# A linear-attention kernel with a gated feed-forward: order and places from tables, narrower carried products, one-pass decay test

## The chip, the cores and the metric

The kernel runs on one core of a Trainium2 chip. A core has a matrix engine (TensorE, called PE in the profile, with its weight loads as PEld), a vector engine (VectorE, DVE), a scalar engine (ScalarE, ACT), GpSimd (POOL) and SyncE (SP), which here issues the transfers. Products are written to PSUM, eight banks of 128 x 512 floats, and read from there by VectorE and ScalarE. Each engine works through its own list of instructions in a fixed order and waits at semaphores. The metric is the time of one execution in microseconds.

## What is computed

```python
def _attn_ref(r, k, v, w, u):                 # 4 x 8 heads x 768 steps x 48
    state = np.zeros((B, H, D, D)); y = np.zeros_like(r)
    for t in range(S):
        kt, vt, rt, wt = (k[:, :, t], v[:, :, t], r[:, :, t], w[:, :, t])
        cur = np.einsum('bhd,bhe->bhde', u[None] * kt, vt)
        y[:, :, t] = np.einsum('bhd,bhde->bhe', rt, state + cur)
        state = wt[:, :, :, None] * state + np.einsum('bhd,bhe->bhde', kt, vt)
    return y

def _moe_ref(x, w_in, conv_w, w_out):         # 4 x 768 x 384, d_ff 1024
    h = np.maximum(x @ w_in, 0.0)
    conv_out = ...                            # along the steps, kernel 3, per channel
    gate = 1.0 / (1.0 + np.exp(-conv_out))
    return (h * gate @ w_out)
```

The result y, with the heads side by side, is the x of the second function. The decays w lie between 0.8 and 0.95. The three weight arrays arrive in double precision; the others are float.

## The kernel before

The 768 steps of each of the four batches are cut into six chunks of 128 steps, 24 chunks n in all. A chunk goes through stage_a and stage_b; a block of 384 steps (two a batch, eight in all) goes through block, once its chunks are there.

stage_a loads w, k, r and v of a chunk and turns w, k and r with PE (`tr`, line 700). VectorE forms running products of the decays (scans, lines 708 and 719) and scales k and r with them, into the tile kr (lines 716, 723). The last 16 of the 48 dimensions of each head sit apart; they are collected into the tile last, by products on line 733 in the first four chunks and by transfers (line 741) later. GpSimd forms r*k*u (z, lines 749, 751) and spreads its sums on the diagonal of the score tile pm (line 755). Line 765 turns the scaled keys back (kh). Two passes of ScalarE test that all decays lie in a safe range (line 774).

stage_b decays the old state s into sd (lines 801 and 804, VectorE) and copies it to sbd (line 809, ScalarE), forms the scores (line 817), copies their upper triangle into pm (line 822), forms the new state (lines 836, 840), and adds up the result in one bank: first the carried part, state times r (`carried`, line 856, in all chunks but the first of a batch), then the part within the chunk (`within`, line 872). The result goes to xT as a float part and a correction (lines 877, 878).

block multiplies by the weights: 64 hidden tiles (line 887: nine products each, three each of three parts), their gating by relu, convolution, sigmoid and product (lines 899 to 909), and 24 output tiles (line 916). Both weights are first converted from double precision, in 17 pieces, each of three operations of ScalarE, two of VectorE (lines 600, 603) and two of GpSimd (lines 605, 585), and are loaded a second time for a range test (lines 620, 623).

Every operation is only recorded (`op`) with the tiles that it reads and writes. Plan.run then lays all of them out with estimated lengths (LEN), ranks (RANKS), costs for a change of shape on PE (SWITCH) and limits on places (CAPS), engine by engine, and Plan.issue writes them out in the order found. Where PE would have nothing to do in the first 120 us of that estimate, it records a filler product (`warm`, line 552: 256 columns of the identity).

## Time and profile before

| | before |
|---|---|
| median of three runs | 382.7 us (381.83 to 382.95) |
| profiled execution | 381.93 us |
| its span, first to last instruction | 380.2 us |
| PE busy, instructions | 97%, 3431 |
| VectorE, ScalarE, GpSimd busy | 72%, 65%, 47% |
| read from and written to memory | 31.88 MB, 4.72 MB |

The profile is one execution. A busy share is the time in which an engine has at least one instruction under way, so side-by-side instructions count once; the mean of one instruction can therefore be longer than the distance between two. The time of a run is somewhat longer than the span.

### The profile page before, as it was taken

How to read it: one execution, taken by the hardware profiler on the slowest of the kernel's cores; microseconds unless marked ns; L12 is line 12 of the kernel's file. 1: busy time of each engine (PE TensorE's matmuls, PEld its weight loads, DVE VectorE, ACT ScalarE, POOL GpSimd, SP SyncE). 2: the span in 40 equal slices, each digit the busy share in tenths (PEclk: the TensorE clock that was granted, in tenths of full speed). 3: DMA queues.
4: the chain of work that ended last, by engine and by line, in shares of the span. 5: the costliest groups of instructions: out<-in, count | busy, mean ns of one | idle time of the engine just before them, and what ended most of it. 6: DMA issues, size and time to landing. Idle time of an engine off the chain costs nothing.

```text
span 380.2 us, 9086 instructions
## 1 busy us (share of the span) xinstructions
PE 368.9 (97%) x3431; PEld 320.4 (84%) x3431; DVE 272.8 (72%) x547; ACT 247.7 (65%) x656; POOL 177.0 (47%) x199
## 2 busy tenths in 40 slices
PE   8999999989999999999999999999999999999993
PEld 5878796878998778789977979898977997999993
DVE  1998699994999588896297576698858487276700
ACT  6464888996798536887377456785654565487821
POOL 6387388998456403464235425355243231234310
PEclk9999999999999999999999999999999999999999
DMA  8999945226553758574235222334512000100011
GB/s 169 256 279 245 229 101 146 86 44 185 123 116 66 178 103 219 114 229 129 56 91 117 44 48 46 71 92 93 114 52 67 0 20 4 41 22 21 22 43 47
DMA packets 113815, 39.24 MB, mean 103 GB/s; under 512 B 102349, under 2 KB 109286, under 8 KB 113766
## 3 DMA queue, kind: packets, MB, share of 16 engines
q1 hardware_dynamic: 113764, 38.61, 41.8%
q8 instruction: 28, 0.46, 0.5%
q14 instruction: 21, 0.17, 0.2%
q10 hardware_dynamic: 2, 0.00, 0.0%
HBM read 31.88 MB, written 4.72 MB: 96 GB/s over the span
## 4 chain that ended last, share of the span: by engine, by line
PE 79%; ACT 7%; DVE 5%; DMA 3%; POOL 3%; issue 2%; SPq 0%; DVEq 0%; POOLq 0%; ACTq 0%
PE bank L887 23%; PE bank L916 23%; PE bank L856 9%; PE bank L817 5%; PE bank L700 5%; PE bank L872 5%; PE bank L836 3%; DMA r<-in_r_dram 2%; PE bank L552 2%; PE bank L765 2%; POOL val L605 1%; PE bank L733 1%; ACT val L596 1%; ACT junk L774 1%; DVE a L901 1%
## 5 line engine op out<-in xcount | busy, mean ns | idle before, releaser
L916 PE MATMUL bank<-wo,gh 128*128 128x384 f32 x576 | 122.1, 345 | 0.3 <-POOL wo L585 0.3
L887 PE MATMUL bank<-xT,wi 128*128 128x386 f32 x576 | 122.0, 346 | 0.3 <-DVE xT L878 0.2
L909 POOL TENSOR_TENSOR gh<-g,gh 128x384 fp32r<-128x384 f32 x64 | 65.5, 1031 | 99.6 <-ACT gh L908 97.4
L887 PEld LDWEIGHTS bank<-xT,wi 128*128 128x128 f32 x576 | 100.1, 189 | 3.8 <-issue 1.5
L916 PEld LDWEIGHTS bank<-wo,gh 128*128 128x128 f32 x576 | 98.8, 188 | 3.1 <-issue 1.7
L901 DVE SCALAR_TENSOR_TENSOR a<-bank,cw,a 128x384 f32<-128x384 f32 x64 | 38.4, 610 | 24.7 <-ACT a L900 24.1
L755 POOL TENSOR_SCALAR_AFFINE_SELECT pm<-dg 128x1024 f32<-128x1024 f32 x24 | 26.7, 1114 | 48.7 <-PE bank L872 38.9
L899 ACT ACTIVATE bank<-bank 128x386 f32<-128x386 f32 x64 | 30.4, 478 | 24.8 <-PE bank L887 24.3
L905 ACT ACTIVATE a<-a 128x384 f32<-128x384 f32 x64 | 33.3, 523 | 16.1 <-DVE a L903 15.9
L906 DVE TENSOR_TENSOR g<-bank,a 128x384 f32<-128x384 f32 x64 | 34.7, 550 | 12.6 <-ACT a L905 11.7
L822 DVE COPY_PREDICATED pm<-upper,bank 128x512 f32<-128x512 int32 x48 | 33.9, 735 | 7.2 <-PE bank L817 7.2
L903 DVE SCALAR_TENSOR_TENSOR a<-bank,cw,a 128x384 f32<-128x384 f32 x64 | 38.3, 610 | 0.7
L900 ACT ACTIVATE a<-bank,cw 128x384 f32<-128x384 f32 x64 | 36.5, 580 | 1.3 <-DVE g L906 0.6
L749 POOL TENSOR_TENSOR z<-r,k 128x384 f32<-128x384 f32 x24 | 24.9, 1037 | 25.9 <-DMA r<-in_r_dram 15.6
L908 ACT CAST gh<-g 128x384 fp32r<-128x384 f32 x64 | 32.0, 511 | 7.2 <-DVE g L906 6.4
L708 DVE TENSOR_TENSOR_SCAN kr<-bank,one_end 128x387 f32<-128x387 f32 x24 | 22.9, 955 | 11.3 <-POOL z L751 6.9
L856 PE MATMUL bank<-kr,sbd 112*64 112x128 f32 (+1 forms) x240 | 29.2, 290 | 0.4 <-DVE pm L822 0.4
L872 PE MATMUL bank<-pm,v 128*32 128x128 f32 x384 | 26.1, 277 | 0.0
L872 PE MATMUL bank<-pm,vz 128*32 128x128 f32 x384 | 25.8, 274 | 0.0
L751 POOL TENSOR_TENSOR z<-z,ubc 128x384 f32<-128x384 f32 x24 | 24.2, 1010 | 1.1
L856 PEld LDWEIGHTS bank<-kr,sbd 112*64 112x64 f32 (+1 forms) x240 | 13.5, 122 | 13.1 <-issue 11.8
L872 PEld LDWEIGHTS bank<-pm,v 128*32 128x32 f32 x384 | 19.6, 109 | 4.5 <-issue 3.8
(103 smaller groups left out, 587.6 us busy)
## 6 DMA issues: line engine op xcount, KB each, us to landing
gh<-in_moe_w_out_dram SPq DMA_DIRECT2D x5, 1152.0 KB, 7.0
w<-in_w_dram SPq DMA_DIRECT2D x24, 192.0 KB, 3.1
k<-in_k_dram SPq DMA_DIRECT2D x24, 192.0 KB, 3.3
r<-in_r_dram SPq DMA_DIRECT2D x24, 192.0 KB, 3.7
v<-in_v_dram SPq DMA_DIRECT2D x24, 192.0 KB, 3.1
gh<-in_moe_w_in_dram SPq DMA_DIRECT2D x4, 1152.0 KB, 7.0
out_dram<-val SPq DMA_DIRECT2D x24, 192.0 KB, 1.9
last<-kr SPq DMA_DIRECT2D x120, 16.2 KB, 1.9
```

The lines of the kernel that those rows point to most:

```text
L822: op("DVE", "cp", lambda g=g: nc.vector.copy_predicated(out=pm.t[:, g], mask=upper.unsqueeze(1).to_broadcast([P, NP, L]), data=sc[g].t.rea ...
L856: nc.tensor.matmul(rows(a, w), lhsT=sbd.t[:, m, e:e + w], rhs=rt(m), start=(j == 0), stop=False, skip_group_check=True)
L872: nc.tensor.matmul(rows(a, 32), lhsT=lhs, rhs=pm.t[:, g, j, :], start=(c == 0 and i == 0), stop=(i == 3), skip_group_check=True)
L887: nc.tensor.matmul(t.t[:, 0:xs.stop - xs.start], lhsT=wi[:, m, a, f * P:(f + 1) * P], rhs=xT[:, x0 + m, c, xs], start=(m == 0 and j == 0), ...
L900: ("ACT", "mul", lambda: nc.scalar.mul(out=a(), in_=h(1), mul=cw[:, 1, fs]), [t, "cw"], [a1]),
L901: ("DVE", "stt", lambda: nc.vector.scalar_tensor_tensor(out=a(), in0=h(0), scalar=cw[:, 0, fs], in1=a(), op0=ALU.mult, op1=ALU.add), [t], ...
L903: ("DVE", "stt", lambda: nc.vector.scalar_tensor_tensor(out=a(), in0=h(2), scalar=cw[:, 2, fs], in1=a(), op0=ALU.mult, op1=ALU.add), [t], ...
L905: ("ACT", "sig", lambda: nc.scalar.activation(out=a(), in_=a(), func=AF.Sigmoid), [], [a1]),
L906: ("DVE", "gate", lambda: nc.vector.tensor_tensor(out=g.t[:, 0:width], in0=h(1), in1=a(), op=ALU.mult), [t, a1], [g]),
L908: ("ACT", "cast", lambda: nc.scalar.copy(out=part(0)[:, 0:width], in_=g.t[:, 0:width]), [g], [key]),
L909: ("POOL", "lo", lambda: nc.gpsimd.tensor_tensor(out=part(1)[:, 0:width], in0=g.t[:, 0:width], in1=part(0)[:, 0:width].bitcast(F32), op=AL ...
L916: nc.tensor.matmul(acc.t[:, 0:DM], lhsT=part(a)[:, tt * P:(tt + 1) * P], rhs=wo[:, f, c, :], start=(f == 0 and a + c == 0), stop=(f == FT ...
```

## The change

It replaces the planner by two tables: ORDER, the numbers of all 2134 operations and of six fillers in the order in which they are issued, and PLACES, which buffer each takes when it is first used. With it:

- the carried products are all of 32 columns, 12 a chunk instead of 8 of 64 or 32;
- one pass of ScalarE per chunk, the square of w - 0.875 from the turned decays in PSUM with its sum, tests the decays, with a copy of three columns per chunk for a test of the chunk's product of decays; four small operations compare both at the end;
- the first part of the decay of the state goes from VectorE to GpSimd (new line 675), the second from VectorE to ScalarE;
- twelve row-sized buffers (strips) serve what had its own: a, g, val, e, z and v; w, k and r share six, s and sd four; the ring of large buffers has six places instead of five; dA has one buffer instead of two; all eight banks serve every use;
- u is spread by a product in the table's order (new line 629).

The core of the diff:

```diff
-        for _, i in order:
-            if not isinstance(i, int):
-                self.warm(i)
-                continue
-            for b in ops[i][4]:
-                if b.kind.make and not b.made:
-                    b.t, b.made = b.kind.make(), True
-            ops[i][2]()
+        done, places = set(), iter(PLACES)
+        for i in ORDER:
+            if i < 0:
+                self.warm(self.spare[-1 - i])
+                continue
+            _, _, f, deps, bufs = self.ops[i]
+            assert deps <= done
             for b in bufs:
                 if b.t is None:
+                    b.t = b.view(b.store[next(places)])
+            f()
+            done.add(i)
...
+ORDER = [
+    231, 51, 0, 1, 4, 276, 435, 235, 194, 2, 232, 236, 55, 190, -8, -8, -8, -8, -8, 237, 52, 20, 238, 233, 239, 5, 6,
...
+        op("ACT", "relu", lambda: nc.scalar.activation(
+            out=junk.t.rearrange("p (m t) -> p m t", t=L), in_=seg(wp.t, 1), func=AF.Square, bias=guard_mid,
+            accum_out=flags[:, n:n + 1]), [wp], [junk])
...
+        op("ACT", "fill", lambda: nc.scalar.copy(out=firsts[:, :, n], in_=kr.t[:, 0, 1:WID:SL]), [kr], [])
...
-        for j, (bias, scale) in enumerate(((guard_hi, 1.0), (guard_lo, -1.0))):
-            op("ACT", "guard", lambda j=j, bias=bias, scale=scale: nc.scalar.activation(
-                out=junk.t, in_=W.t[:, :, 0:D], func=AF.Relu, bias=bias, scale=scale, accum_out=flags[:, 2 * n + j:2 * n + j + 1]),
-                [W], [junk], )
...
-            op("DVE", "sd", lambda: nc.vector.tensor_tensor(
+            op("POOL", "psd", lambda: nc.gpsimd.tensor_tensor(
                 out=sd.t[:, 0:KT], in0=old.t[:, 0:KT], in1=kr.t[0:R, 0, 1:WID:SL].unsqueeze(2).to_broadcast([R, KT, D]),
-                op=ALU.mult), [old, kr], [sd], port=True)
-            op("DVE", "small", lambda: nc.vector.tensor_scalar(
-                out=sd.t[:, KT], in0=old.t[:, KT], scalar1=last.t[:, 0, 1:2], scalar2=None, op0=ALU.mult),
-                [old, *lasts], [(sd, 1)], [sd, last], port=True)
+                op=ALU.mult), [old, kr], [sd])
+            op("ACT", "fill", lambda: nc.scalar.mul(out=sd.t[:, KT], in_=old.t[:, KT], mul=last.t[:, 0, 1:2]),
+               [old, *lasts], [(sd, 1)], [sd, last])
...
             def carried():
-                for j, at in enumerate(range(0, H * D, P)):
-                    a = at
-                    while a < at + P:
-                        m, e = divmod(a, 2 * D)
-                        w = min(64 if a % 64 == 0 else 32, 2 * D - e)
-                        nc.tensor.matmul(rows(a, w), lhsT=sbd.t[:, m, e:e + w], rhs=rt(m), start=(j == 0), stop=False,
-                                         skip_group_check=True)
-                        a += w
+                for a in range(0, H * D, 32):
+                    m, e = divmod(a, 2 * D)
+                    nc.tensor.matmul(rows(a, 32), lhsT=sbd.t[:, m, e:e + 32], rhs=rt(m), start=(a < P), stop=False,
+                                     skip_group_check=True)
...
-    fsum = fconst.tile([P, 1], F32, name="fsum")
-    nc.vector.tensor_reduce(out=fsum, in_=flags, axis=AX.X, op=ALU.add)
-    nc.tensor.matmul(banks[0][0:1, 0:1], lhsT=fsum, rhs=ones_f[:, 0:1], start=True, stop=True)
+    nc.vector.tensor_tensor(out=ok, in0=flags, in1=limits, op=ALU.is_le)
+    nc.vector.tensor_scalar(out=high, in0=firsts.rearrange("p m n -> p (m n)"), scalar1=LEAST, scalar2=None, op0=ALU.is_ge)
+    nc.vector.tensor_reduce(out=fsum, in_=ok, axis=AX.X, op=ALU.min)
+    nc.vector.tensor_reduce(out=fsum2, in_=high, axis=AX.X, op=ALU.min)
+    nc.tensor.matmul(banks[0][0:1, 0:1], lhsT=fsum, rhs=fsum2, start=True, stop=True)
```

Three places of the new order, before and after. First, PE around the carried products of the second chunk (line 856 before, 723 after; the last number is the product's shape, columns of the weights first; L700 and L584 are transposes, L836 and L707 the new state, L872 and L738 the part within the chunk, L646 the transpose of the keys back). Before:

```order
L836 MATMUL bank_68<-v_127,kh_157 48x48
L856 MATMUL bank_65<-kr_134,sbd_143 64x128
L856 MATMUL bank_65<-kr_134,sbd_143 32x128 x2
L856 MATMUL bank_65<-kr_134,sbd_143 64x128 x2
L856 MATMUL bank_65<-kr_134,sbd_143 32x128
L856 MATMUL bank_65<-last_140,sbd_143 32x128
L856 MATMUL bank_65<-last_140,sbd_143 64x128
L700 MATMUL bank_66<-ident,r_124 128x128 x3
L700 MATMUL bank_71<-ident,w_121 128x128 x3
```

After, the same place, with the third chunk's set behind the second's:

```order
L707 MATMUL bank_64<-strip_127,kh_162 48x48
L646 MATMUL bank_69<-ident,kr_140 128x128 x3
L723 MATMUL bank_65<-kr_141,sbd_149 32x128 x9
L723 MATMUL bank_65<-last_146,sbd_149 32x128 x3
L584 MATMUL bank_66<-ident,nat_132 128x128 x3
L723 MATMUL bank_64<-kr_139,sbd_150 32x128 x9
L723 MATMUL bank_64<-last_145,sbd_150 32x128 x3
L738 MATMUL bank_65<-pm_159,strip_125 32x128
L738 MATMUL bank_65<-pm_159,vz_154 32x128
```

Eight products of two widths have become twelve of one, and the second and third chunk's sets stand with one transpose between them, followed by the products within the chunk, which are 32 columns wide too.

Second, PE at the start (L473 and L364 warm on a tile of zeros, L552 and L441 are the fillers on the identity). Before, around the first transpose of loaded data:

```order
L552 LDWEIGHTS ident
L552 MATMUL bank_66<-ident 128x256
L552 LDWEIGHTS ident
L552 MATMUL bank_66<-ident 128x256
L700 MATMUL bank_64<-ident,w_120 128x128 x3
L552 LDWEIGHTS ident
L552 MATMUL bank_66<-ident 128x256
```

After, from the fourth of the five fillers on:

```order
L441 LDWEIGHTS ident
L441 MATMUL bank_71<-ident 128x256
L441 LDWEIGHTS ident
L441 MATMUL bank_71<-ident 128x256
L584 MATMUL bank_67<-ident,nat_131 128x128 x3
L629 MATMUL bank_71<-ubc,ones_f 128x384
L584 MATMUL bank_64<-ident,nat_132 128x128 x3
L584 MATMUL bank_69<-ident,nat_133 128x128 x3
```

Thirty fillers stood ahead of the first transpose and more behind it; now there are five, and the next real product follows directly.

Third, the decay of the state. Before, on VectorE in the second chunk (L801 and L804 the decay, L600 and L603 conversion, L708 a scan, L842 the first state):

```order
L842 COPY s_162<-bank_69 112x192
L801 TENSOR_TENSOR sd_160<-s_162,kr_134 112x144
L600 TENSOR_SCALAR bank_71<-gh 128x384
L600 TENSOR_SCALAR bank_70<-gh 128x384
L603 ISA val_72<-bank_71,val_72 128x768
L603 ISA val_73<-bank_70,val_73 128x768
L708 SCALAR_TENSOR_TENSOR kr_135<-bank_66,one_end 128x387
L600 TENSOR_SCALAR bank_69<-gh 128x384
L714 RECIPROCAL dA_129<-kr_135 128x3
L804 TENSOR_SCALAR sd_160<-s_162,last_140 112x48
```

After, on GpSimd in the third and fourth chunk (L675 the decay, L494 and L474 conversion, L633 z, L637 the diagonal of pm):

```order
L633 TENSOR_TENSOR strip_122<-strip_122,ubc 128x384
L637 AFFINE_SELECT pm_159<-dg_158 128x1024
L474 TENSOR_TENSOR wi<-strip_119,wi 128x384
L675 TENSOR_TENSOR sd_168<-sd_167,kr_139 112x144
L474 TENSOR_TENSOR wi<-strip_128,wi 128x384
L494 TENSOR_TENSOR strip_124<-strip_124,strip_126 128x384
L474 TENSOR_TENSOR wi<-strip_129,wi 128x384
L675 TENSOR_TENSOR sd_166<-sd_165,kr_140 112x144
```

The decay has left VectorE's list and stands in GpSimd's between operations of full width.

## Rows read from the trace of the kernel before

**Rows 1.** The page, busy time, share and instructions of each engine.
```profile
PE 368.9 (97%) x3431; PEld 320.4 (84%) x3431; DVE 272.8 (72%) x547; ACT 247.7 (65%) x656; POOL 177.0 (47%) x199
```

**Rows 2.** Stretches: from:to, length, busy us of each engine, clock, DMA share, GB/s.
```profile
core 0: us, PE busy (x) PEld busy (x) DVE busy (x) ACT busy (x) POOL busy (x), PEclk, DMA share, GB/s
0.00:47.00 47.00, 45.13 (x520) 35.26 (x520) 33.86 (x81) 28.49 (x91) 28.13 (x52) 1.00 0.96 235
47.00:100.00 53.00, 50.92 (x410) 43.23 (x411) 45.78 (x92) 46.24 (x124) 45.16 (x47) 1.00 0.43 110
60.00:80.00 20.00, 18.48 (x158) 14.85 (x155) 19.85 (x38) 18.98 (x51) 17.91 (x20) 1.00 0.35 93
100.00:374.40 274.40, 272.82 (x2503) 241.88 (x2501) 193.00 (x376) 172.54 (x443) 103.70 (x101) 1.00 0.34 80
```

**Rows 3.** Stretches, of line 552 (fillers) alone.
```profile
0.00:47.00 47.00, 14.38 (x96) 9.91 (x96) 1.00 0.96 235
47.00:100.00 53.00, 7.12 (x45) 4.07 (x45) 1.00 0.43 110
```

**Rows 4.** Timeline of PE, four places: start, length, instruction.
```profile
1.19 1.78 PE L473 MATMUL bank<-junk 128*128 128x384 bf16 x5 [1.19 <-DVE table L477]
...
8.88 0.49 PE L700 MATMUL bank<-ident,w 128*128 128x128 f32 x3
...
46.48 0.42 PE L887 MATMUL bank<-xT,wi 128*128 128x386 f32 x1
...
374.20 0.19 PE L979 MATMUL bank<-ones_f,fsum 128*1 128x1 f32 x2
```

**Rows 5.** Timeline of PE, one carried set and one set of line 872.
```profile
142.31 1.34 PE L856 MATMUL bank<-kr,sbd 112*64 112x128 f32 x11
...
144.05 0.79 PE L916 MATMUL bank<-wo,gh 128*128 128x384 f32 x3
...
145.10 0.30 PE L872 MATMUL bank<-pm,v 128*32 128x128 f32 x1
...
145.91 0.27 PE L872 MATMUL bank<-pm,v 128*32 128x128 f32 x1
146.11 0.55 PE L700 MATMUL bank<-ident,w 128*128 128x128 f32 x3
```

**Rows 6.** Groups by form: busy us, mean ns of one, idle time before.
```profile
L872 PE MATMUL bank<-pm,v 128*32 128x128 f32 x384 | 26.1, 277 | 0.0
...
L801 DVE TENSOR_TENSOR sd<-s,kr 112x144 f32<-112x144 f32 x20 | 9.7, 486 | 0.2
L804 DVE TENSOR_SCALAR sd<-s,last 112x48 f32<-112x48 f32 x20 | 9.1, 457 | 1.0 <-ACT last L736 0.9
...
L600 DVE TENSOR_SCALAR bank<-gh 128x384 int32<-128x384 int32 x14 | 7.5, 547 | 0.0
...
L774 ACT ACTIVATE junk<-w,guard_lo 128x384 bf16<-128x384 f32 x24 | 14.8, 617 | 0.2
...
L774 ACT ACTIVATION_READ_ACCUMULATOR junk<-w,guard_lo 128x1 f32 x24 | 4.6, 193 | 0.0
...
L749 POOL TENSOR_TENSOR z<-r,k 128x384 f32<-128x384 f32 x24 | 24.9, 1037 | 25.9 <-DMA r<-in_r_dram 15.6 <-DVE dA L714 5.1 <-DVE a L903 2.7
...
L579 POOL TENSOR_TENSOR val<-val,e 24x128 f32<-24x128 f32 x1 | 0.5, 459 | 5.1 <-DVE val L577 5.1
```

**Rows 7.** The chain that ended last, four pieces: start, us, what.
```profile
2.97 3.41 PE bank L552 x16
...
7.41 1.63 PE bank L552 x14
...
122.02 0.72 PE bank L916 x3
...
177.72 9.38 PE bank L916 x54
```

**Rows 8.** Timeline of VectorE, its first scan and the fourth correction.
```profile
9.47 0.96 DVE L708 TENSOR_TENSOR_SCAN kr<-bank,one_end 128x387 f32<-128x387 f32 x1 [6.94 <-POOL z L751]
...
46.48 0.53 DVE L878 TENSOR_TENSOR xT<-bank,xT 128x384 fp32r<-128x384 f32 x1
```

More of the change, by code (lines that the diff above doesn't have):

```diff
@@ L18 @@
 PSUM = bass.MemoryType.PSUM
-W_LO, W_HI = 0.75, 1.05
+W_MID, W_SPREAD = 0.875, 2.25
+LEAST = 2.0 ** -44
 BANKS = 8
-GH = 5
+GH = 6
+STRIPS = 12
 WARM = 5
-DOWN = 1.6
-PREFER = 10.0
 EARLY = 4
-COLD, WARM_LEN, WARM_END = 8.0, 0.14, 120.0
-CAPS = (4, 5, 3, 3, 4)
-GT, TB = 1, 1
-LEN = dict(
-    tr=0.332, kback=0.373, scores=0.82, carried=0.68, state=0.475, y=0.9, mm3=0.531,
-    scan=0.875, small=0.1, pad=0.07, kt=0.465, dg=0.44, cp=0.62, sd=0.3, s=0.265,
-    stt=0.527, gate=0.465, wts=0.461, wstt=0.461,
-    range=1.25, rtest=0.8, fill=0.172, kh=0.335, guard=0.61, sbd=0.364, relu=0.41, mul=0.475, sig=0.426, cast=0.418, out=0.375,
-    exp=0.48, z=0.97, diag=1.06, lo=0.966,
-    gather=1.6, load=0.57, issue=0.48, spread=0.64,
-)
@@ L81 @@
[L81 to L85 removed]
+ORDER = [
[103 rows of a table added]
+]
+PLACES = [
[24 rows of a table added]
+]
 class Buf:
     def __init__(self, kind):
[L92 removed]
@@ L95 @@
[L95 to L111 removed]
+        self.store, self.view = kind
@@ L208, in run @@
-    def run(self, ranks):
-        self.reset()
-        ops, n = self.ops, len(self.ops)
-        left = [len(o[3]) for o in ops]
-        engines = ("PE", "DVE", "ACT", "POOL", "SP")
-        ready = {e: [] for e in engines}
-        free = dict.fromkeys(engines, 0.0)
-        locked = dict(DVE=0.0, POOL=0.0)
-        wire = Wire(("SP", "ACT"))
-        for i in range(n):
-            if not left[i]:
-                heapq.heappush(ready[ops[i][0]], (ranks[i], i))
-        events, order, t, end, mode = [], [], 0.0, 0.0, FULL
-        def places(bufs):
-            taken = []
+        self.ops.append((eng, name, f, deps, bufs))
@@ L952, in rwkv_conv_moe_kernel @@
     for n in range(N):
-        plan.at("load", n)
         loads(n)
```

364 lines of the change are left out of this document (75 added, 289 removed), and 130 rows, old and new, of tables (ORDER, PLACES, hidden).

## Prediction

> **What bounds the kernel now.** I read the page's busy line first, then stretches of the span, then the chain of waits, then single rows. The matrix engine (PE) is busy for 97% of the 380.2 us, the others for 47% to 72% [rows 1]. That sounds like a kernel bound by PE throughout, but the stretches divide it in two [rows 2]. From 100 us to the last product at 374.4 PE is busy for 272.82 of 274.4 us, so each product that gets shorter there should shorten the end. Before 100 us the busy share misleads: 141 filler products of line 552 take 21.50 us, all of it there [rows 3]. They compute nothing; the old planner puts one in wherever it has no real product to give.
>
> So I count useful PE time. Until 47 us PE is busy for 45.13 [rows 2], less 14.38 of fillers [rows 3], less 1.78 for the five warming products [rows 4]: 29.0, so 18.0 us are lost. From 47 to 100 it is 50.92 less 7.12, 43.8, so 9.2 are lost. That is 27.2 us of loss in the opening, 1.6 between 100 us and the last product, and 5.8 of copy, transfer and closing after it. What remains of 380.2 is 345.6 us of useful products. The profiled execution took 381.93, 1.7 above its span, and the runs' median is 382.7, 0.8 above that; I add these 2.5 at the end.
>
> **Term 1, the carried products: -19.7 us.** Line 856 issues 8 products a chunk, of 64 and 32 columns mixed, recorded as 16 instructions. One set begins at 142.31 and the next kind of product at 144.05: 1.74 us, 109 ns an instruction [rows 5]. The products of line 872 are all of 32 columns and go round the four column strips of the engine: 32 instructions from 145.10 to 146.11, 1.01 us, 32 ns each, although a single one takes 277 [rows 5, 6]. So products of one width of 32 run side by side and the mixed set runs nearly one after another. The changed set has 12 products, 24 instructions, in strip order, with the same 128 moving columns: 24/32 of 1.01 is 0.76 us. Twenty chunks (all but each batch's first) at 1.74 - 0.76 = 0.98 give 19.7. Bounds: if nothing runs side by side, 24 x 109 ns = 2.6 us and +17; if the set's closing delay falls away too, 24 x 26 ns (the 0.81 us between the first and the last start on line 872, over 31 steps) and -22. I take the row of like shape.
>
> The Trainium skill ("TensorEngine Tiling (Array Packing)", Key Properties) says that a change of tiling mode, not of tile alone, drains the engine. By that rule a set that mixes widths drains within itself and a set of one width does not, which 109 against 32 ns bear out; the sum would be the same by it.
>
> **Term 2, fewer changes of shape: -5 us.** A group of three large products takes 0.52 us among its own kind (54 instructions in 9.38) and 0.72 where a narrow kind follows [rows 7]. The two orders list 34 such places before and 20 after: 14 x 0.2 = 2.8. A set of 32-column products stands directly behind another of that width at 20 places, before at none. The last of line 872's instructions starts at 145.91 and the next kind at 146.11, 0.20 us where the steps inside are 0.026 [rows 5]; if such a pair saves 0.15 of that, 20 give 3. I take -5; bounds -2 and -6. Useful products: 345.6 - 19.7 - 5 = 321.
>
> **Term 3, fillers and the opening: -4 us.** Of 141 fillers 6 are left. Taking 20.6 us of them out gives nothing by itself, since they stand where PE had no work; what counts is the 27.2 us of loss that they cover. Of these, 8.9 pass before the first transpose, when the first load has landed [rows 4]; that stays. Both orders have the same real products ahead of the first hidden product (17 transposes, 5 transposes back, 4 gathers, scores, states and results, 3 carried). What releases that product is the fourth correction of xT on VectorE, at 46.48 to 47.01 [rows 8]. From its first scan at 9.47 VectorE has 70 operations up to there, in the new order 64: seven decays of the state fewer (0.457 to 0.486 each), nine conversion operations more (0.547), a scan, a reduction, a reciprocal, a state sum and four short memsets fewer [rows 6]. That is about the same work, so the first hidden product stays near 47 us, with 18 us lost.
>
> Behind it the old kernel loses another 9.2. VectorE (19.85 of 20), ScalarE (18.98) and GpSimd (17.91) are nearly full from 60 to 80 us [rows 2], because weights are still being converted. The new order has begun 8 conversions by 47 us instead of 4 (4 x 1.09 us of VectorE less to come, two operations of 0.547 each), and VectorE no longer decays the state (0.94 a chunk, about four chunks here). That takes 8 us from VectorE where it is full; I let it return 4 of the 9.2, since ScalarE and GpSimd are near their limits too. Loss of the opening: 23; bounds 18 (all 9.2 returned) and 28.
>
> **Term 4, the decay test: 0 by itself.** 48 passes of 617 ns with 48 accumulator reads of 193 ns (38.9 us of ScalarE [rows 6]) become 24 of each and 24 copies of 3 columns. Those cost between nothing and 0.6 us each: 5 to 19 us less on ScalarE. After 100 us that lies on an engine busy for 172.5 of 274.4 us [rows 2], and PE doesn't wait for it; in the opening it is part of what term 3 returns. The four small operations of the final test come ahead of the last product; without that cover they would add under 1 us. I charge 0.2.
>
> **Term 5, the state's decay goes to GpSimd: +0.9 us.** No row shows this product there. One of 384 columns takes 1037 ns, one of 128 columns on 24 partitions 459 [rows 6]; 144 columns are nearer the second, so 0.5, and 20 make 10 us on an engine busy for 103.7 of 274.4 after 100 us. Queued behind it are z, pm and the low halves of gh; for it wait ScalarE's copies to sbd and then the carried products. I put the later loss at 2.5 instead of 1.6; bounds 0.5, and 18 if in each of 16 later chunks one operation of 1.04 us ahead of it in the queue is paid in full.
>
> **Term 6, the clock in the opening: +2 us.** 16 fillers of 256 columns from 2.97 us on take 3.41, which is 213 ns each and 1.2 GHz; 14 from 7.41 on take 1.63, 116 ns each, close to 2.4 GHz [rows 7]. (The column of the granted clock says 1.00 throughout; here the spacing decides.) PE had been given products without a pause since 1.2 us. In the new order ten warming products end at about 4 us (five like those before, which end at 2.97, and five of 213 ns), and PE stands still until 8.9, so the first chunks probably start at 1.2 GHz. PE has slack there (29 us of work before 47), so I charge 2 us for the longer chain of the first chunks; bounds 0 and 16 (the rival below).
>
> Shared buffers, the sixth place in the ring and one dA instead of two do no work; they cost something only where an instruction waits for a place, which terms 3 and 5 bound. Loads ahead of the fourth chunk's v grow from 16 to 20, 0.8 MB or 3 us at the 235 GB/s of that stretch [rows 2]; VectorE's work until 47 us covers them, and without that cover it is 3 us.
>
> **Sum:** products 321, opening 23 and 2, later loss 2.5, end 6: 354.5 of span, and 2.5 more make **357 us**.
>
> **Rivals.**
> - *The clock stays low until the hidden products (0.13).* Then up to 29 us of products take twice as long from 8.9 us on, the first hidden product starts near 63 instead of 47, +16 less the 2 charged: 371. For it speaks the 213 ns row; against it that the products are then nearly continuous, as they were from 1.2 to 6.4 us when the clock rose. The Trainium skill ("TensorE: Matmul & The Clock Gate", Why this matters for your kernels) speaks for this rival: it warns against idle gaps between bursts, and this change removes what filled them.
> - *PE waits for the decay on GpSimd (0.08).* Term 5's upper bound: 373.
> - *The opening gives nothing back (0.10).* Loss 28: 362. For it: three engines full at once.
> - *Slower: the 32-column products don't run side by side in this set (0.04).* Twenty times 2.6 instead of 0.76: 394. It decides from 2.0 us a set on (25.7/20 above 0.76). Against it: line 872's 1.01.
> - *No change (0.05).* Another engine paces the rest and PE idles for what it saves: 382. Against it: VectorE at 193.0 of 274.4 after 100 us.
> - *The opening is packed fully (0.05).* 18 lost there, nothing for the clock, nothing more after 100 us: 349 or less.
>
> The forecast gets 0.55, with 350 to 364 as its own range. A measurement of this kernel can tell about 0.3% (1.1 us) from no change. Faster by more: 0.92; within: 0.02; slower: 0.06. The range of 346 to 372 leaves out the slower and the unchanged case, most of GpSimd's and a third of the clock's.
>
> **What would show it.** Term 1: line 723 with 24 instructions in some 0.76 us a chunk. Term 2: large groups followed less often by 0.72. Term 3: first hidden product at 44 to 50 us, useful PE time of some 75 us until 100 us, VectorE over nine tenths from 47 to 80. Term 5: under 2 us of waits of line 723 for sbd. Term 6: the first transposes at 9 us at half rate, soon after at full. I am wrong if a carried set takes over 1.2 us, if PE waits over 6 us after 100 us, or if the first hidden product comes after 53.

## Result and the profile after

| | before | after |
|---|---|---|
| median of 4 runs | 382.26 us | 342.79 us (342.08 to 343.83) |
| after / before | | 0.897, 95% interval 0.894 to 0.900 |
| span of the profiled execution | 380.2 us | 342.1 us |

The kernel is 39.5 us faster. The direction was forecast, the size was not: 357 was predicted, with 346 to 372.

The page of the changed kernel, busy time of each engine (beside [rows 1]), and the stretches (beside [rows 2]; from:to, length, busy us, clock, DMA share, GB/s):

```profile
PE 332.0 (97%) x3456; PEld 307.0 (90%) x3456; DVE 261.0 (76%) x508; ACT 237.8 (70%) x652; POOL 181.7 (53%) x221
```

```profile
0.00:47.00 47.00, 43.72 (x493) 35.31 (x494) 39.67 (x92) 34.37 (x105) 38.57 (x69) 0.96 0.78 206
47.00:100.00 53.00, 52.61 (x511) 48.54 (x510) 50.37 (x98) 47.81 (x137) 44.16 (x47) 1.00 0.78 189
60.00:80.00 20.00, 19.89 (x179) 18.62 (x178) 18.90 (x37) 17.88 (x53) 17.39 (x19) 1.00 0.74 187
100.00:335.90 235.90, 234.27 (x2447) 222.09 (x2446) 170.34 (x317) 153.72 (x409) 99.00 (x106) 1.00 0.33 79
```

The share of PE is 97% as before, and again it doesn't say where the time went. The same stretches for the fillers alone (line 441, beside [rows 3]):

```profile
0.00:47.00 47.00, 1.56 (x6) 0.85 (x6) 0.96 0.78 206
47.00:100.00 53.00, 0.00 (x0) 0.00 (x0) 1.00 0.78 189
```

Counted as in the prediction, useful PE time up to 47 us is 43.72 - 1.78 - 1.56 = 40.4, so 6.6 are lost instead of 18.0. From 47 to 100 us 0.4 are lost instead of 9.2, later 1.6. The last large product ends at 336.8, 0.9 us behind the last of these stretches, so the tail is 5.3. What remains of 342.1 is 328.2 us of products. Beside the sum of the prediction:

| | predicted | measured |
|---|---|---|
| products | 321 | 328.2 |
| loss of the opening, clock included | 25 | 7.0 |
| later loss | 2.5 | 1.6 |
| tail | 6 | 5.3 |
| run beyond span | 2.5 | 0.7 |

So by this count the products gave 7 us less than forecast, and the opening 18 us more. The count takes off too much for the fillers, here and in the prediction: their recorded times overlap those of the products beside them (in the kernel before, a filler takes 125 ns from its start to the next instruction's, 17.7 us for all 141, and not the 21.50 of [rows 3]). The time until 100 us in which no real product is under way falls from 20.0 to 6.4 us. By that count the opening gave 13.6 us where 2.2 were forecast, and the products 24.0 where 24.7 were. By either count it is the opening that the forecast missed.

Timeline of PE (beside [rows 4]), its start and its first hidden products:

```profile
1.19 1.78 PE L364 MATMUL bank<-junk 128*128 128x384 bf16 x5 [1.19 <-DVE table L368]
2.76 1.27 PE L441 MATMUL bank<-ident 128*128 128x256 bf16 x5
3.85 0.90 PE L584 MATMUL bank<-ident,nat 128*128 128x128 f32 x3
...
9.29 0.88 PE L646 MATMUL bank<-ident,kr 128*128 128x128 f32 x3
...
10.94 0.55 PE L646 MATMUL bank<-ident,kr 128*128 128x128 f32 x3 [0.28 <-DVE kr L599]
...
39.77 7.80 PE L752 MATMUL bank<-xT,wi 128*128 128x386 f32 x42
```

The first transpose starts at 3.85 instead of 8.88, the first hidden product at 39.77 instead of 46.48, and 14 groups of three follow each other without a break. VectorE between its first scan and that product, in the kernel before and in the changed one:

```profile
9.47:46.48 37.01, 31.82 (x69) 1.00 0.99 253
```

```profile
5.55:39.77 34.22, 30.80 (x62) 0.95 0.95 258
```

The 6.7 us that the first hidden product comes earlier are 3.9 of an earlier first scan (5.55 against 9.47 [rows 8]), 1.0 less of work and 1.8 less of standing still (3.4 instead of 5.2).

Groups of the changed kernel (beside [rows 6]): the carried products, the decay on GpSimd, the pass of the decay test and the copy of 3 columns:

```profile
L723 PE MATMUL bank<-kr,sbd 112*32 112x128 f32 x360 | 16.3, 277 | 0.1
...
L675 POOL TENSOR_TENSOR sd<-sd,kr 112x144 f32<-112x144 f32 x20 | 8.6, 431 | 15.2 <-DVE sd L711 9.7 <-DVE sd L713 5.4
```

```profile
L591 ACT ACTIVATE junk<-bank,guard_mid 128x384 bf16<-128x384 f32 x24 | 13.9, 578 | 9.4 <-PE bank L584 3.8 <-DVE kr L594 3.8 <-DVE kr L602 1.7
...
L601 ACT COPY firsts<-kr 128x3 f32<-128x3 f32 x24 | 4.6, 199 | 0.0
```

Line 723 waits 0.1 us in all, so the carried products do not wait for the decay on GpSimd, which takes 431 ns. Two pieces of the chain of waits show a carried set of 24 instructions (beside [rows 5], where a set took 1.74):

```profile
30.72 0.80 PE bank L723 x24
...
103.30 0.66 PE bank L723 x24
```

### The profile page after: what moved, and what is told of

Same layout as the page of the kernel before. It is cut to its first block, busy times and chain, and to the rows that moved or that the text cites. A ratio compares the mean times of both kernels' runs of the same rounds, so it can differ in the third digit from the quotient of the medians.

```text
span 342.1 us, 9231 instructions
## 1 busy us (share of the span) xinstructions
PE 332.0 (97%) x3456; PEld 307.0 (90%) x3456; DVE 261.0 (76%) x508; ACT 237.8 (70%) x652; POOL 181.7 (53%) x221
## 4 chain that ended last, share of the span: by engine, by line
PE 78%; DVE 8%; ACT 7%; issue 2%; DMA 2%; SPq 1%; ACTq 0%; DVEq 0%
PE bank L781 26%; PE bank L752 24%; PE bank L584 7%; PE bank L690 6%; PE bank L738 6%; PE bank L723 4%; PE bank L707 3%; PE bank L646 2%; DVE kr L594 2%; DMA last<-kr 1%; ACT bank L764 1%; ACT strip L765 1%; SPq L623 1%; DVE kr L602 1%; ACT junk L591 1%
## 5 line engine op out<-in xcount | busy, mean ns | idle before, releaser
L774 POOL TENSOR_TENSOR gh<-strip,gh 128x384 fp32r<-128x384 f32 x64 | 64.3, 1015 | 85.3 <-ACT gh L773 81.4
L766 DVE SCALAR_TENSOR_TENSOR strip<-bank,cw,strip 128x384 f32<-128x384 f32 x64 | 38.9, 610 | 22.9 <-ACT strip L765 22.6
L770 ACT ACTIVATE strip<-strip 128x384 f32<-128x384 f32 x64 | 33.3, 523 | 25.7 <-DVE strip L768 25.4
L771 DVE TENSOR_TENSOR strip<-bank,strip 128x384 f32<-128x384 f32 x64 | 34.7, 551 | 14.4 <-ACT strip L770 13.5
L584 PE MATMUL bank<-ident,nat 128*128 128x128 f32 x216 | 38.5, 294 | 2.5 <-ACT nat L578 2.1
L768 DVE SCALAR_TENSOR_TENSOR strip<-bank,cw,strip 128x384 f32<-128x384 f32 x64 | 38.9, 614 | 1.2
L765 ACT ACTIVATE strip<-bank,cw 128x384 f32<-128x384 f32 x64 | 36.9, 580 | 2.2 <-DVE strip L771 0.4
L773 ACT CAST gh<-strip 128x384 fp32r<-128x384 f32 x64 | 32.5, 512 | 7.7 <-DVE strip L771 7.6
L584 PEld LDWEIGHTS bank<-ident,nat 128*128 128x128 f32 x216 | 27.1, 148 | 10.2 <-ACT nat L578 3.7
L637 POOL TENSOR_SCALAR_AFFINE_SELECT pm<-dg 128x1024 f32<-128x1024 f32 x24 | 26.2, 1092 | 13.8 <-DVE dg L634 11.4
L738 PE MATMUL bank<-pm,strip 128*32 128x128 f32 x384 | 25.0, 275 | 0.0
L633 POOL TENSOR_TENSOR strip<-strip,ubc 128x384 f32<-128x384 f32 x24 | 24.5, 1024 | 0.7
L738 PE MATMUL bank<-pm,vz 128*32 128x128 f32 x384 | 24.8, 273 | 0.0
```

The lines of the kernel that those rows point to most:

```text
L584: nc.tensor.transpose(out=cols(m), in_=src.t[:, 2 * m:2 * m + 2, :].rearrange("p h d -> p (h d)"), identity=ident)
L738: nc.tensor.matmul(rows(a, 32), lhsT=lhs, rhs=pm.t[:, g, j, :], start=(c == 0 and i == 0), stop=(i == 3), skip_group_check=True)
L765: ("ACT", "mul", lambda: nc.scalar.mul(out=a(), in_=h(1), mul=cw[:, 1, fs]), [t, "cw"], [a1]),
L766: ("DVE", "stt", lambda: nc.vector.scalar_tensor_tensor(out=a(), in0=h(0), scalar=cw[:, 0, fs], in1=a(), op0=ALU.mult, op1=ALU.add), [t], ...
L768: ("DVE", "stt", lambda: nc.vector.scalar_tensor_tensor(out=a(), in0=h(2), scalar=cw[:, 2, fs], in1=a(), op0=ALU.mult, op1=ALU.add), [t], ...
L770: ("ACT", "sig", lambda: nc.scalar.activation(out=a(), in_=a(), func=AF.Sigmoid), [], [a1]),
```

## Experiments

Where a ratio is given, it is to the kernel before, which ran on the same chip, with its 95% interval.

### Parts of the change in the order of before

**Narrow carried products alone.** The kernel before with the changed kernel's loop in place of the mixed one, nothing else:

```diff
-                for j, at in enumerate(range(0, H * D, P)):
-                    ...
-                        w = min(64 if a % 64 == 0 else 32, 2 * D - e)
-                        nc.tensor.matmul(rows(a, w), lhsT=sbd.t[:, m, e:e + w], ...
+                for a in range(0, H * D, 32):
+                    m, e = divmod(a, 2 * D)
+                    nc.tensor.matmul(rows(a, 32), lhsT=sbd.t[:, m, e:e + 32], ...
```

> The kernel before with the carried products in 32 columns and nothing else. Terms 1 and 2 of the prediction for this part: 20 sets at 0.76 instead of 1.74 us, 19.7 us less, and nothing of the 5 us for fewer changes of shape, since the order is as before: 362.6, with 361 to 364. Rival (part of it lies where PE waits for others, in the opening): two or three sets lie ahead of 47 us, so 17 less, 365. If the whole difference of after beyond this is the opening, the rest of 20 us has to come from the fillers, the order and the relief of other engines.

Measured: 367.15 us, 0.962 (0.956 to 0.969), 14.3 less, short of the forecast and of the rival. In the trace the distance from each PE instruction's start to the next one's, summed by kind, falls from 35.2 to 15.9 us for the carried products, 19.3 as expected; the state products beside them rise from 11.3 to 13.7. That leaves 16.9, and the profiled execution took 364.88, 17.1 less than the 381.93 of the kernel before. The median lies 2.3 higher: of the four runs the two of 364.9 and 365.8 have a granted clock of 0.999, the two of 368.6 and 369.0 one of 0.995 and 0.992. The first hidden product starts at 42.68, so the shorter sets in the opening do count there.

**No fillers.**

```diff
             if not isinstance(i, int):
-                self.warm(i)
                 continue
```

> The kernel before without any of its 141 fillers; the order of all real work is as before. Premise of the prediction (fillers stand only where PE has nothing to do): first transpose still at 8.9 us, first hidden product near 46.5, time 382 (381 to 383). Rival A (PE takes its list strictly in order, so a filler that is already in the list delays the real product behind it): the 30 fillers ahead of the first transpose cost about 5.0 us (3.41 + 1.63 in the profile of before), so it starts at 4 to 5 us, the first hidden product near 41, and the time is 374 to 378. Rival B (the clock falls without the fillers): first chunks at half rate, first hidden product after 50, time 385 or more.

Measured: 384.38 us, 1.007 (1.004 to 1.009). The first transpose moves to 4.48, as rival A has it, but the first hidden product stays at 46.33. Stretches of this run, columns as above:

```profile
20.00:30.00 10.00, 6.77 (x59) 4.50 (x57) 6.42 (x16) 5.86 (x19) 9.92 (x11) 0.66 1.01 274
50.00:60.00 10.00, 7.46 (x43) 6.09 (x43) 9.08 (x21) 9.54 (x25) 10.00 (x12) 0.86 0.54 133
60.00:70.00 10.00, 9.42 (x58) 7.24 (x54) 6.80 (x15) 6.74 (x19) 5.91 (x7) 0.63 0.50 145
```

PE is busy for 6.77 and 7.46 us of the first two stretches; its longest wait, 3.2 us, ends at 24.0. The granted clock is 0.66 in the first and 0.63 behind the second, means between the levels of 1.2 and 2.4 GHz, and 0.975 over the whole span instead of 0.998. The fillers delay products (next run) and hold the clock, and in the old order the two are nearly even. The Trainium skill ("TensorE: Matmul & The Clock Gate", Why this matters for your kernels) warns of idle gaps between bursts; this run agrees: without what fills the gaps the kernel is 0.7% slower.

**No fillers ahead of the first transpose.**

```diff
-                self.warm(i)
+                if begun:
+                    self.warm(i)
                 continue
+            begun = begun or ops[i][0] == "PE"
```

> The kernel before without the 30 fillers that stand ahead of the first transpose; the other 111 stay. Premise of the prediction: 382, first transpose at 8.9. Rival A: first transpose at 4 to 5 us; the first hidden product 2 to 5 us earlier (fillers that stay may give some of it away again), time 377 to 380. Rival B (clock): first transposes at half rate and no gain, 382 or more.

Measured: 379.66 us, 0.993 (0.990 to 0.997). The timeline of PE:

```profile
4.47 0.90 PE L703 MATMUL bank<-ident,w 128*128 128x128 f32 x3
5.17 2.98 PE L555 MATMUL bank<-ident 128*128 128x256 bf16 x13
7.94 0.85 PE L703 MATMUL bank<-ident,k 128*128 128x128 f32 x3
...
44.24 0.42 PE L890 MATMUL bank<-xT,wi 128*128 128x386 f32 x1
```

So it was the fillers, not the load, that held the first transpose until 8.88. Of 4.4 us gained there, the next 13 fillers take back a part, 2.2 reach the first hidden product and 1.8 the end.

**Everything but the order and the buffers, with five fillers.** Narrow products as above, and:

```diff
-                self.warm(i)
+                if kept < 5:
+                    self.warm(i)
+                    kept += 1
...
-            op("DVE", "sd", lambda: nc.vector.tensor_tensor(
+            op("DVE", "sd", lambda: nc.gpsimd.tensor_tensor(
...
-            op("DVE", "small", lambda: nc.vector.tensor_scalar(
+            op("DVE", "small", lambda: nc.scalar.mul(
...
-        for j, (bias, scale) in enumerate(((guard_hi, 1.0), (guard_lo, -1.0))):
+        op("ACT", "guard", lambda: nc.scalar.activation( ... bias=guard_hi, scale=1.0, ...
+        op("ACT", "guard", lambda: nc.scalar.copy(out=firsts[:, :, n], in_=W.t[:, 0:KT, 0]), [W], [junk])
```

> The kernel before, in its own order and with its own buffers, with every other part of the change: 5 fillers only, carried products in 32 columns, the state's decay on GpSimd and its 16-row part on ScalarE, one pass of the decay test and a copy of 3 columns in place of the second pass (this leaves out the lower bound of the decays). Theory A (the gain beyond the carried products is the fillers' place in PE's list and the relief of VectorE and ScalarE): 343 to 348. Theory C (it is the order and the places of the buffers): 353 to 360, little below the run with narrow carried products and without the lead.

Measured: 368.71 us, 0.966 (0.960 to 0.971): no better than narrow products alone. Theory A falls; it is also above the 353 to 360 of theory C.

**The same with all 141 fillers** (the first piece of that diff left out).

> The kernel before in its own order, with its 141 fillers, and with narrow carried products, the decay on GpSimd, its 16-row part on ScalarE and one pass of the decay test with a copy of 3 columns in place of the second (this leaves out the lower bound of the decays). Beside the run with narrow products alone (367.2) it is what terms 4 and 5 bring in the old order. The prediction's term 3 let 4 us of the loss behind 47 us return through them: 363. Rival (in the old order other waits set the opening and the relief brings nothing): 366 to 368.

Measured: 367.05 us, 0.964 (0.961 to 0.967), against 367.15 without the relief. In the old order terms 4 and 5 bring nothing that shows beside intervals of some 3 us: the first hidden product starts at 42.13 instead of 42.68, and from 47 to 100 us PE is busy for 49.03 us instead of 50.16, with the same fillers.

### The order

The next four kernels are the changed one with another table in `ORDER`; the place of a buffer is the one that came free first instead of the next in `PLACES`:

```diff
...
+            for b in bufs:
+                left[id(b)] -= 1
+                if not left[id(b)]:
+                    stores[id(b.store)].append(b.place)
```

> All of the changed kernel's instructions and buffers, but issued in the order of the kernel before, with its 141 fillers at their places (places given out first come, first served). Theory O (most of what the narrow carried products don't explain is the order of the opening): little below the kernel before with narrow carried products, whose median was 367: 361 to 367. Rival P (the other parts, the larger ring and the shared buffers give it whatever the order): 343 to 352.

> The changed kernel's order up to its 78th group of three large products (there at about 100 us), then everything else in the order of the kernel before; instructions and buffers are those of the changed kernel. From the traces, the stretch from 100 us to the last large product is 257 us in the kernel before with narrow carried products and 237 in the changed one, of which 12 is work that the changed one had done by 100 us; 8 is order. Theory O: 342.8 and 8 make 351 (348 to 354), with the opening as in the changed kernel. Rival Q (the gain lies in fewer changes of shape in the rest): 358 or more.

> The reverse: the order of the kernel before, with its fillers, up to its 78th group of large products, then everything else in the changed kernel's order. Theory O: the opening's 12 us stay lost, 342.8 and 12 make 355 (353 to 360). Rival Q: 350 or less. If both halves add up, this run and the one with the changed opening lie together as far above 342.8 as the run in the old order throughout.

> The changed kernel in its own order, but each buffer's place is the one that came free first instead of the one in the table. If the table of places does nothing beyond the order: 342.8 (342 to 344). If places matter (an instruction waits for a place whose last reader is late): 345 or more.

| order | us | ratio (interval) |
|---|---|---|
| old throughout | 375.79 | 0.988 (0.984 to 0.992) |
| new opening, old rest | 358.22 | 0.943 (0.937 to 0.949) |
| old opening, new rest | 369.89 | 0.971 (0.966 to 0.975) |
| new throughout | 343.41 | 0.903 (0.897 to 0.909) |

The last one takes as long as the changed kernel, so the table of places adds nothing that first come, first served doesn't. The other three are slower than theory O allowed (361 to 367, 348 to 354, 353 to 360), and the new opening with the old rest lies at the 358 of rival Q; the old opening with the new rest, 369.89 where rival Q had 350 or less, speaks against that rival. The old opening costs 27 us, the old rest 15, each with a seam. The stretch behind the seam, of the new opening and then of the old one:

```profile
100.00:130.00 30.00, 26.43 (x398) 21.40 (x397) 21.73 (x43) 16.61 (x53) 14.98 (x16) 0.94 0.46 111
```

```profile
100.00:130.00 30.00, 25.23 (x285) 22.68 (x287) 21.65 (x43) 19.36 (x53) 11.89 (x14) 0.94 0.54 146
```

In the changed kernel PE is busy for 30.00 of the same 30 us, in the old order throughout for 29.70, so 3.6 and 4.8 us are nearly all the seam's own, and the halves needn't add up (27 and 15 against 33 for the old order throughout). The opening holds the larger part, as theory O says. Without the seams both parts are larger than its 12 and 8 us. That the old order does worse here than with the buffers of before (375.79 against 367.05) was not taken further.

### Parts taken out of the changed kernel

**Mixed carried products** in the new order: the first diff of the experiments, reversed.

> The changed kernel with the carried products in 64 and 32 columns mixed, as before; order, buffers and all else as changed. Theory T1 (term 1: a set of one width costs about 1 us less, and it stands beside another set of 32 columns): 20 sets at 1.74 instead of 0.72 us give 20.4, and up to 3 more where a set of 32 columns no longer has a neighbour of its width: 342.8 and 20 to 24 make 363 to 367. Rival (as much as the narrow products brought in the order of before, 14 us by the medians): 357.

Measured: 359.54 us, 0.941 (0.938 to 0.945): 16.7 more than the changed kernel, between the two theories; the carried products take 33.3 us from start to start instead of 14.9.

**30 fillers ahead of the first transpose.**

```diff
-    ... 190, -8, -8, -8, -8, -8, 237, ...
+    ... 190, (30 times -8), 237, ...
```

> The changed kernel with 30 fillers ahead of its first transpose instead of 5. Theory A (fillers in PE's strict list delay real products, and VectorE's work from its first scan to the first hidden product sets the opening): about 4 us later with the first transpose (near 7.9 us) and with the first hidden product (near 43.5), time 345 to 347. Rival (the opening has slack, or the clock that the fillers raise gives it back): 342 to 343.5.

Measured: 344.98 us, 0.903 (0.900 to 0.906), 2.2 more, at the lower edge of theory A. The timeline shows the delay of 4.3 us, and that the transposes then run at the full rate, 0.49 instead of 0.90 us for three:

```profile
2.77 5.52 PE L441 MATMUL bank<-ident 128*128 128x256 bf16 x30
8.13 0.49 PE L584 MATMUL bank<-ident,nat 128*128 128x128 f32 x3
```

The profiled execution is the longest of the six (348.43, with a granted clock of 0.988 where the others have 0.998 to 1.000). In it the first hidden product starts at 44.6 instead of 39.8, and nearly all of that reaches the end: its span is 346.7 instead of 342.1. Where the other executions stood at the first hidden product no trace shows.

**Terms 4 and 5 taken back.**

```diff
-            op("POOL", "psd", lambda: nc.gpsimd.tensor_tensor(
+            op("POOL", "psd", lambda: nc.vector.tensor_tensor(
...
-            op("ACT", "fill", lambda: nc.scalar.mul(
+            op("ACT", "fill", lambda: nc.vector.tensor_scalar(
...
-        op("ACT", "relu", lambda: nc.scalar.activation(
...
+        def passes():
+            for twice in range(2):
+                nc.scalar.activation(
...
```

> The changed kernel with terms 4 and 5 taken back: the state's decay and its 16-row part on VectorE (20 of each), and the pass of the decay test done twice on ScalarE (24 more of 0.6 us; the copy of 3 columns stays). Theory A (after 100 us both lie beside PE's work; before it VectorE is nearly full, with about five chunks there, 5 times 0.9 us of VectorE): 344 to 348. Rival Z (term 4's and term 5's 0: other engines have slack): 342 to 343.5. Rival G (the decay on GpSimd cost PE time, as term 5's upper bound has it): under 342.

Measured: 360.81 us, 0.943 (0.939 to 0.946): 18.0 more, over three times the most that theory A allowed, where the prediction had 0 and 0.9. The first hidden product starts at 43.0, 3.2 us late; most of the rest arises behind it. The stretch from 100 to 330 us in the changed kernel and in this run, in which PE stands idle for 1.6 and for 8.5 us:

```profile
100.00:330.00 230.00, 228.37 (x2413) 216.19 (x2412) 170.15 (x316) 152.29 (x406) 97.98 (x106) 1.00 0.34 81
```

```profile
100.00:330.00 230.00, 221.51 (x2396) 204.06 (x2395) 176.98 (x339) 151.76 (x412) 90.84 (x90) 1.00 0.35 83
```

The longest sum of waits in that stretch stands ahead of the transposes, for ScalarE's copies into `nat` (0.3 us in the changed kernel):

```profile
PE bank L584 <- ACT nat L578: 1.8, 3, 1.0
```

Four kernels take this apart: the decay alone, the twofold pass over the bank alone, and two in which the second pass reads something else.

> The changed kernel with the state's decay and its 16-row part back on VectorE, at the places in the program that they have on GpSimd and ScalarE. In the run that took back both terms ScalarE waited 9 us for them (sbd). Theory S: 0.9 us more a chunk on VectorE, which is over nine tenths busy until 66 us, so 4 to 10 us: 347 to 353. Rival Z (only the opening's five chunks and half hidden): 342 to 345.

Measured: 349.75 us, 0.918 (0.916 to 0.920), 7.0 more. Taking the decay off VectorE (its larger part to GpSimd, the 16-row part to ScalarE) is worth 7 us in the new order. ScalarE's copies to sbd wait 9.1 us for it in this run:

```profile
ACT sbd L682 <- DVE sd L678: 9.1, 10, 1.8
```

Here the first hidden product starts at 38.79, earlier than in the changed kernel (39.77), so what this run loses arises behind it.

> As the run with a second pass over the loaded tile, but both passes read the bank that VectorE's two scans read. In the run that took back terms 4 and 5 together VectorE's scans waited 12.5 us for the passes, and not in the changed kernel. Theory B (the bank is the link: engines that read one bank take turns): above the run with the pass over the loaded tile, by 3 us or more. Rival (only ScalarE's time counts): the same as that run.

The run over the loaded tile, against which this forecast is set, comes last. The pass over the constant tile:

```diff
+            nc.scalar.activation(out=junk.t, in_=one_end[:, 0:H * D], func=AF.Square, bias=guard_mid,
+                                 accum_out=spare_sum[:, 0:1])
```

> The changed kernel with a second pass on ScalarE behind each pass of the decay test, over a constant tile that no other engine needs (its sum is used nowhere): ScalarE's time alone, without the bank and without the loaded tile. Theory B (in the run with both passes on the bank, 357, the bank was the link: VectorE's scans waited 13 us there for the passes): 344 to 350. Rival S (ScalarE's time alone): 355 to 359, the scans then waiting as long for the delayed first passes.

Measured: 357.04 us, 0.938 (0.935 to 0.940), and 356.72 us, 0.934 (0.930 to 0.938). These are the pass over the bank twice and the second pass over a constant tile (which VectorE's scans read too, and which is written only at the start). The two are the same within their intervals, so the bank is not the link and theory B falls: a second pass costs 14 us by the time that it takes on ScalarE. With the decay's 7 that would be 21 for both, where 18 were measured. Waits of PE in the run with the pass over a constant tile, its first hidden product and two stretches:

```profile
PE bank L585 <- ACT nat L579: 6.9, 8, 1.9
PE bank L727 <- ACT sbd L686: 1.4, 3, 0.9
```

```profile
47.82 0.42 PE L756 MATMUL bank<-xT,wi 128*128 128x386 f32 x1
```

```profile
20.00:24.00 4.00, 4.00 (x20) 4.00 (x20) 4.00 (x9) 0.85 (x5) 3.20 (x4) 0.50 1.15 308
...
28.00:47.00 19.00, 16.73 (x270) 13.71 (x272) 14.14 (x29) 14.83 (x48) 13.49 (x16) 0.82 0.75 203
```

Behind each pass of 0.62 us and its read of 0.19 stand ScalarE's small copies into `nat` (line 579), for which the transposes wait: 6.9 us instead of 2.1. PE then runs short of work, the clock halves (0.50 from 20 to 24 us), and the first hidden product is 8 us late. The other 6 us arise behind it: from 100 to 330 us PE is idle for 5.8 us instead of 1.6. With both passes over the bank the first hidden product starts at 42.8, 5 us earlier than here, PE is idle for 7.0 us in that stretch, and the median is the same. So the delay of the first hidden product alone does not give the time.

With `in_=W.t[:, :, 0:D]` in place of the constant tile:

> The changed kernel with a second pass of the decay test on ScalarE, which reads the loaded tile as the passes of before did, not the bank (its sum is used nowhere). Theory S (each list is now packed for these durations, so 0.8 us more a chunk on ScalarE is passed on to PE in the opening, where ten chunks lie): 346 to 352. Rival Z (term 4's 0: ScalarE has slack): 342 to 343.5.

Measured: 367.79 us, 0.964 (0.962 to 0.967). That is far above theory S (346 to 352), but this run doesn't test term 4: the extra pass waits for later loads that the table has put into the same place (ScalarE's test waits 4.8 us at once for a load of r). It shows only that the table frees a loaded tile as soon as the pass of the kernel no longer needs it.

### Small additions

```diff
-    ... 476, 58, 217, ...
+    ... 476, 58, (15 times -5), 217, ...
```

> The changed kernel with 15 fillers where PE waits from 22.1 to 23.9 us, and nothing else of the three small things tried together. Term 6 by this: the trace of the changed kernel shows 3.4 us at half the clock from 24.0 us on; if the wait brings that, the fillers hold the clock and save up to 1.7 us: 341 to 342.2. Rival: 342.8, since VectorE paces this part.

Measured: 342.22 us, 0.897 (0.895 to 0.900), 0.6 less, which can't be told from no change. The stretches of the changed kernel, and of this one:

```profile
20.00:24.00 4.00, 2.23 (x50) 1.81 (x50) 4.00 (x8) 2.99 (x12) 4.00 (x5) 1.00 1.05 340
24.00:28.00 4.00, 4.00 (x38) 3.17 (x38) 2.13 (x5) 3.94 (x12) 3.15 (x4) 0.57 1.10 295
```

```profile
20.00:24.00 4.00, 3.88 (x65) 3.39 (x66) 3.70 (x7) 3.52 (x13) 4.00 (x5) 1.00 1.01 322
24.00:28.00 4.00, 4.00 (x51) 3.38 (x49) 3.25 (x7) 3.90 (x13) 2.61 (x4) 1.00 0.94 274
```

In this execution the clock holds from 24 to 28 us (1.00 instead of 0.57), and three transposes at 23.92 take 0.49 us instead of 0.83. That the fillers did it is not shown: it also holds there in two runs of the new order without them (places first come, first served; the decay back on VectorE), after waits of 1.45 and 1.56 us instead of 1.77, and one of the four runs of the changed kernel has a mean granted clock of 1.000. That run took 342.22, as much as the median here. Nor does VectorE pace these chunks once the clock has fallen: from 24 to 28 us it is busy for 2.13 us of the four, PE for all four.

With these fillers and two things more:

```diff
+        past = n % NCH == NCH - 1
-        op("PE", "kback", k_back, [kr], [tb])
+        op("PE", "kback", (lambda: None) if past else k_back, [kr], [tb])
...
-    ok, high = strips[0][:, 0:N + 6], strips[1][:, 0:KT * N]
+    ok, high = one_end[:, 0:N + 6], one_end[:, P:P + KT * N]
```

> The changed kernel with three small things: 15 fillers where PE waits from 22.1 to 23.9 us, after which the trace shows half the clock for 3.4 us; no transposes back, and no copies of them, in the last chunk of each batch, where nothing reads them; and the final test in a tile of its own instead of two strips whose transfer to memory it waits for. Theory: up to 1.7 us from the clock, 4 times 0.3 from the transposes, 0.9 from the test: 339 to 341.5. Rival (the waits move elsewhere): 342.8.

Measured: 341.40 us, 0.894 (0.891 to 0.897), the lowest median of the study, 1.4 below the changed kernel; the intervals overlap. The final test starts its last step at 335.5 us instead of 338.6, since it no longer waits for the transfer of a strip. In the two traces the time from the end of the last large product to the end of the span is 4.4 us instead of 5.3, and that product ends 1.45 us earlier; which of the three things brings what is not shown.

## Why the prediction was right and wrong

**The step that failed** is in terms 3 and 4: "That is about the same work, so the first hidden product stays near 47 us, with 18 us lost", 4 us of the 9.2 behind it returned, and "0 by itself" for the decay test. VectorE's work was nearly the same (31.8 and 30.8 us), but the first hidden product came 6.7 us earlier and the loss from 47 to 100 us went from 9.2 to 0.4, so that the opening lost 7.0 us where 25 were forecast. I weighed each engine's work by itself and asked whether it had slack. The runs show a product of two things, all with narrow carried products:

| | without terms 4 and 5 | with them |
|---|---|---|
| old order | 367.2 | 367.1 |
| new order | 360.8 | 342.8 |

Each order stands there with its own fillers and buffers; with the buffers and the relief of the changed kernel the old order takes 375.8, so the shared buffers are not what brings the gain. The relief brings nothing in the old order and 18 us in the new one; the order brings 6 without the relief (a little more, perhaps, had the table been made for it, since the decay stands there at places meant for GpSimd) and 24 with it. The mechanism is strict lists: PE, VectorE and ScalarE each work in a fixed order, so 0.8 us ahead of a copy on ScalarE delays the transposes, the scans and the next chunk, however much of the engine's time is idle on average. Nor does this end with the opening, as term 4 has it ("and PE doesn't wait for it"): without the relief PE is idle for 8.5 us from 100 to 330 us, with it for 1.6, and of 17.3 us between the two spans only 3.2 lie ahead of the first hidden product.

**The fillers.** "Taking 20.6 us of them out gives nothing by itself" held in sum (0.7% slower). Its reason did not: the first transpose stood behind 30 fillers, not behind the load, and starts at 4.5 without them.

**Term 1** was right in mechanism and near in size: 19.7 predicted, 19.3 and 18.4 in the traces, 14.3 and 16.7 in the medians. In the old order the state products take back 2.4 us beside the narrow sets; the rest of the difference goes with the lower clock of two of the four runs, which no run tests by itself. **Term 2** was too large. From 100 us on the out products fall from 186.2 to 183.8 ns from start to start and the hidden ones from 185.6 to 185.5; the narrow sets beside their like go from 33.0 to 30.3. Over all instructions after 100 us that is some 2.7 us (1.2, 0 and 1.0, and 0.5 for line 738), not 5. Of the 7 us by which products were longer than forecast, some 5 can be the half rate of the opening, which counts as product time (an estimate: half of the 6.5 us from the first transpose to 10.4, where the spacing becomes that of the full rate, and of the 3.4 from 24.0).

**Term 5**: no wait, as forecast; but moving the decay off VectorE was itself worth 7 us. **Term 6**: the first transposes run at half rate, as forecast, but PE does not stand still until 8.9: they start at 3.85, and three transposes still take 0.88 us at 9.29 and 0.55 at 10.94. Another 3.4 us at half clock follow from 24.0 on. What this cost against the 2 us charged was not measured; the fillers at 22 us bring 0.6, not to be told from nothing. (In the rival on the clock 8.9 and twice 29 would give 67, not 63.) Of term 4's words the final test fell too: its operations don't come ahead of the last product, they wait for a transfer. Of the rivals, the fully packed opening ("349 or less", 0.05) is the one that came true in its time, and the opening went beyond its 18 us.

**Not settled**: how the 24 us of the new order divide between its single moves, why the relief brings nothing in the old order, and why the shared buffers do worse in the old order.

## What to carry to other kernels

When a hand-made or searched order is replaced together with the work on the engines, do not price the pieces apart: run the durations through the new lists, engine by engine, to the end: here most of what the relief is worth in the new order arose behind the first product that the rest waits for. An engine that is idle for a third of the time still sets the end if its instruction stands ahead of a copy that the matrix engine waits for. Work put in only to fill a fixed list delays the next real product wherever that is ready sooner than planned.

## What was unexpected of the hardware

In the profiled execution of the changed kernel a wait of 1.77 us on PE was followed by some 3.4 us at half the clock (a mean of 0.57 from 24 to 28 us is 1.0 for 0.6 us and 0.5 for 3.4); after waits of 1.45 and 1.56 us at the same place two other runs show 1.00. The first three transposes of the changed kernel took 0.90 us where the column of the clock says 1.00, and three take 0.49 in the run with 30 fillers ahead of them. The trace holds no record of the clock before 10.39 us, and the column counts that time as 1.00; there only the spacing tells the rate. Narrow carried products made the state products beside them dearer (35.3 to 42.8 ns an instruction from start to start).
